# A hand-ordered head for an attention and MLP block: staged weights, stepwise transposes, sliced MLP weights

## The chip, the cores and the metric

The kernel runs on one core of a Trainium2 chip. The metric is the device time of one launch in microseconds, and smaller is better. The engines are called as the profile calls them: PE (TensorE), DVE (VectorE), ACT (ScalarE), POOL (GpSimd) and SP (SyncE, which here issues nearly all DMAs).

## The reference

```python
x = A_x                                   # 1 x 2048 x 640
xn = _layernorm(x)
return x + _A_ref(xn, A_wqkv, A_wo) + _B_ref(xn, B_w1, B_b1, B_w2, B_b2)

def _A_ref(x, wqkv, wo):                  # 32 heads of 20
    q, k, v = split(x @ wqkv)
    p = softmax(q k^T * 20 ** -0.5)
    return (p v) @ wo

def _B_ref(x, w1, b1, w2, b2):            # 640 -> 1536 -> 640
    y = _layernorm(x)
    return _gelu(y @ w1 + b1) @ w2 + b2
```

Everything is float32. An attention block and an MLP block run on the same normalized tokens, and both are added to the input.

## The kernel before, in words

The kernel has two stages. In the *head*, tokens are normalized, transposed and projected to q, k and v, and all weights are prepared. In the *attention* stage, scores, exponentials and products with v run while the MLP and the output projection are fed in between in small pieces, in an order written out by hand (`tc.manual_schedule()`).

A float32 operand is held as a pair of float16 halves, high and low, and a product is three float16 passes (`PASS`). To split a weight matrix, its squares are summed on ACT (`squares`, L94), the sum over partitions is taken by an fp32 product with a matrix of ones on PE (`mxp`, L107, in `pow2`), a power of two is made of it by six small operations on DVE, and then `split` scales (ACT, L128), casts (DVE, L129) and subtracts (DVE, L130), row by row. The matrix wqkv is loaded to one tile `wt` and split in its own place; so are w1 (`w1t`) and w2 (`w2t`) of the MLP.

The head works on four chunks `c` of 512 tokens. For each chunk there are:

- `load_x`: four tiles `xt` of 128 tokens (five buffers in all).
- `norm` (L201 to L214): statistics and scaling on DVE; the two inverse roots come from POOL (`pow`, L186) with a Newton step on DVE. A row of scales goes to `rscr`.
- `transp` (L231 to L236): 20 transposes on PE into PSUM tiles `pt`; ACT takes the high half, DVE the low half, into `xnt`, which also goes to `xscr` in DRAM for the MLP.
- `qk` (five steps `tt`, L252): 30 products into a PSUM tile `qkp`. ACT and DVE evacuate it into a buffer `qkhl` (L261, L262; two buffers), DVE squares it (`sq`, L264), and SP stores the two halves to `qkscr` (L266).
- `lengths` (L287): eight small products of `sq` for each step, from which the largest lengths of q and k are taken; `shifts` turns them into the shifts of the exponents (`brow`, `bscr`) in chunk 3.
- `vproj` (four tiles, L316): 30 products each into `vp`, evacuated into `vfull`.

`qkp`, `pt`, `vp`, and later the scores, share three PSUM buffers (tag `s`).

`residual` (L218, L219) copies x to `accscr` in DRAM and then adds b2 with an accumulating DMA issued by POOL. It stands in the text at the head of chunk 2. In the head the order of the text is no order of the engines: a planner sorts the instructions of each engine by its own estimates. So w1 is prepared in the text after chunk 1, w2 after chunk 2 (`prep`), while the planner may put their parts and the residual elsewhere.

At the end of the attention stage, `finish` of the last unit adds the two parts of its output (L639), multiplies, splits and stores them (`oscr`), with `W1` and `W2` counting the steps of the output projection (`z`, L803, evacuated at L764) that are put in between in the written order. The projection works on pieces of 256 tokens; pieces 4 to 7 need the last unit.

Of the kernel before, what the change touches and what calls it, by code (L numbers as in the profile page):

```python
# [42 lines left out]
def mha_mlp_kernel(tc, x, wqkv, wo, w1, b1, w2, b2, out):  # L43
# [4 lines left out]
    with (  # L48
# [52 lines left out]
        def pow2(acc, tag):  # L101

            lo = keep.tile([P, 1], F32, name=f"lo_{tag}")
            hi = keep.tile([P, 1], F32, name=f"hi_{tag}")
            pt = psS.tile([P, 2, 512], F32, tag="s", name="mxp")[:, 0, :]
            n = acc.shape[1]
            nc.tensor.matmul(pt[:, :n], ones, acc, start=True, stop=True)  # L107
# [11 lines left out]
        def prep(tag, ws, junk):  # L119
            pw[tag] = pow2(squares(ws, junk), tag)  # L120
            s = keep.tile([P, 1], F32, name=f"s_{tag}")
            nc.vector.tensor_scalar(s, pw[tag][1], 4096.0, None, ALU.mult)
            return s

# [8 lines left out]
        with tc.tile_pool(name="pa", bufs=2) as pa, tc.tile_pool(name="pa1", bufs=1) as pa1:  # L133
            wt = pa1.tile([P, KD, 3 * D], F32, name="wt")
            wv = wt.bitcast(F16).rearrange("p k (q s n) -> p k q s n", q=3, s=2)
# [9 lines left out]

            load_x(0)
            for q in range(2):
                for k0, k1 in ((0, 3), (3, KD)):
                    nc.sync.dma_start(wt[:, k0:k1, q * D : (q + 1) * D], wqkv_v[:, k0:k1, q * D : (q + 1) * D])
            nc.sync.dma_start(wt[:, :, 2 * D :], wqkv_v[:, :, 2 * D :])  # L150
            load_x(1)
            make_identity(nc, ident)
            nhalf = keep.tile([P, 4], F32, name="nhalf")
            half = keep.tile([H, 1], F32, name="half")
            nc.gpsimd.memset(nhalf, -0.5)
            nc.gpsimd.memset(half, 0.5)
            nc.gpsimd.memset(ones, 1.0)
# [20 lines left out]
            nc.gpsimd.memset(brow, KROW)  # L178
            nc.sync.dma_start(bscr[H : H + 1, :], brow[0:1, :])
            nc.sync.dma_start(b1t, b1.rearrange("(k p) -> p k", p=P))  # L180
            nc.sync.dma_start(w1t, w1.rearrange("(k p) n -> p k n", p=P))
            nc.sync.dma_start(w2t, w2.rearrange("(k p) n -> p k n", p=P))

            def rsqrt(dst, v, pref):
                t = pa.tile([P, 4], F32, tag=pref + "t", name=pref + "t")
                nc.gpsimd.tensor_tensor(dst, v, nhalf, ALU.pow)  # L186
# [5 lines left out]
            def norm(c):  # L192
# [11 lines left out]
                rsqrt(r, ve, "a")  # L204

                nc.vector.tensor_mul(ve, r, r)
                nc.vector.tensor_mul(ve, ve, mv[:, :, 1])
                nc.vector.tensor_scalar(ve, ve, EPS, None, ALU.add)
                nc.vector.tensor_scalar(r, r, 1024.0, None, ALU.mult)
                for j in range(4):  # L210
                    nc.vector.tensor_scalar(xt[j], xt[j], mv[:, j, 0:1], r[:, j : j + 1],
                                            ALU.subtract, ALU.mult)
                rsqrt(r2, ve, "b")
# [9 lines left out]
            def transp(c):  # L223
                xt = xts.pop(c)
                xnt = pa.tile([P, KD, 2, 512], F16, tag="xnt", name=f"xnt{c}")
                for k0 in range(0, KD, 2):
                    nk = min(2, KD - k0)
                    pt = psS.tile([P, 2, 512], F32, tag="s", name="pt")
                    for k in range(nk):
                        for j in range(4):  # L230
                            nc.tensor.transpose(pt[:, k, j * P : (j + 1) * P],  # L231
                                                xt[j][:, (k0 + k) * P : (k0 + k + 1) * P], ident)
                    ks = slice(k0, k0 + nk)
                    nc.scalar.activation(xnt[:, ks, 0, :], pt[:, :nk], AF.Copy)
                    nc.vector.tensor_sub(xnt[:, ks, 1, :], pt[:, :nk], xnt[:, ks, 0, :])
                nc.sync.dma_start(xscr[:, :, :, c * 512 : (c + 1) * 512], xnt)  # L236
                xnts[c] = xnt
# [3 lines left out]
            norms = []  # L241

            def qk(c, tt):
                xnt = xnts[c]
                ps = psS.tile([P, 2, 512], F32, tag="s", name="qkp")
                for i in range(2):
                    m = 2 * tt + i
                    q, mm = divmod(m, KD)
                    n = 0
                    for k in range(KD):  # L250
                        for a, b in PASS:
                            nc.tensor.matmul(ps[:, i, :], wv[:, k, q, a, mm * P : (mm + 1) * P],  # L252
                                             xnt[:, k, b, :], start=(n == 0), stop=(n == 3 * KD - 1))
                            n += 1
                hl = stp.tile([P, 2, 2, 512], F16, tag="ks", name="qkhl")
# [8 lines left out]
                nc.vector.tensor_mul(sq, hl[:, 0], hl[:, 0])  # L264
                for s in range(2):
                    nc.sync.dma_start(  # L266
                        qkscr[s, 2 * tt * P : (2 * tt + 2) * P, c * 512 : (c + 1) * 512]
                        .rearrange("(i p) t -> p i t", p=P), hl[:, s])

                for i in range(2):  # L270
                    q, mm = divmod(2 * tt + i, KD)
                    if mm == 0:
                        if q == 0:
                            norms.clear()
                            norms.append(psO.tile([P, 512], F32, tag="o", name="norms"))
                            norms.append(psM.tile([P, 512], F32, tag="m", name="norms"))
                    pend.append((norms[q], mm, sq, i, q, c))

            pend = []

            def lengths(last=0):
                todo = pend[: len(pend) - last]
                del pend[: len(todo)]
                for ns, mm, sq, i, q, c in todo:
                    for r in range(4):

                        nc.tensor.matmul(ns[32 * r : 32 * r + 32, :P], heads[:, mm, :],  # L287
                                         sq[:, i, r * P : (r + 1) * P], start=(mm == 0), stop=(mm == KD - 1),
                                         skip_group_check=True)
                    if mm == KD - 1:  # L290
                        nc.vector.tensor_reduce(lmx[:, q, c : c + 1], ns[:, :P], AX.X, ALU.max)
# [16 lines left out]
            def vproj(c, js):  # L308
                xnt = xnts[c]
                for j in js:  # L310
                    ps = psS.tile([P, 2, 512], F32, tag="s", name="vp")
                    for hf in range(2):
                        n = 0
                        for k in range(KD):
                            for a, b in PASS:
                                nc.tensor.matmul(ps[:, hf, :320], xnt[:, k, a, j * P : (j + 1) * P],  # L316
                                                 wv[:, k, 2, b, hf * 320 : (hf + 1) * 320],
                                                 start=(n == 0), stop=(n == 3 * KD - 1))
                                n += 1
                    kb = 4 * c + j  # L320
                    pv_ = ps[:, :, :320].rearrange("p f (h d) -> p f h d", d=DH)
                    vs = (V16 if SPLIT[kb] else V32)[:, kb].rearrange("p (f h) d -> p f h d", f=2)
                    nc.scalar.activation(vs[:, :, :, :DH], pv_, AF.Copy, scale=2.0**-14)  # L323
                    if SPLIT[kb]:
                        nc.vector.scalar_tensor_tensor(vs[:, :, :, VW : VW + DH], pv_, 2.0**-14, vs[:, :, :, :DH],
                                                       ALU.mult, ALU.subtract)

            qks = pa1.tile([P, 2], F32, name="qks")
            junk = pa1.tile([P, 3 * D], BF16, name="junk")

            def prep_qkv(q):
                c0, c1 = q * D, (q + 1) * D
                s = prep("qkv"[q], [wt[:, 0:3, c0:c1], wt[:, 3:, c0:c1]], junk)
                if q < 2:
                    nc.vector.tensor_scalar(qks[:, q : q + 1], pw["qkv"[q]][0], QKTOP, 2.0**-22, ALU.min, ALU.mult)
# [3 lines left out]
            norm(0)  # L339
            transp(0)  # L340
            prep_qkv(0)
            for c in range(4):
                if c + 2 < 4:
# [3 lines left out]
                for tt in range(3):  # L347
                    if c == 0 and tt == 2:
                        prep_qkv(1)
                        norm(1)  # L350
                    qk(c, tt)
                    lengths(2)
                if c == 0:
                    prep_qkv(2)
                if c + 1 < 4:
                    transp(c + 1)
                for tt in range(3, 5):
                    qk(c, tt)
# [633 lines left out]
```

## Time and profile before

| | us |
|---|---|
| median of 3 runs | 1438.71 (1435.95 to 1442.88) |
| profiled execution | 1444.0 |
| its span | 1442.3 |

| engine | busy us | share of the span | instructions |
|---|---|---|---|
| PE | 1348.2 | 93% | 11607 |
| DVE | 1066.4 | 74% | 1445 |
| ACT | 1122.4 | 78% | 1277 |
| POOL | 22.0 | 2% | 60 |

One execution on the chip was taken by the hardware profiler; the span goes from its first to its last instruction. In the rows that follow, a group of instructions is given as line, engine, operation, output and inputs by the kernel's names, shapes, count, busy time, mean ns of one, and the idle time of the engine just before them with what ended it. A row of a timeline begins with its start and duration. A row of a table of stretches has start and end, length, and then for each engine the busy time and the count, the granted clock of PE, the share of the DMA engines and GB/s. A row of waits says who waited for whom: total us, times, the longest. PEld is the loading of weights into PE. The digits of the page are tenths in 40 slices of the span.

### The profile page before, as it was taken

The page shows a single profiled execution, that of the slowest core. Times are in us where ns is not written, and L with a number is a line of the kernel's source. Part 1 is how long each engine was busy: PE and PEld are TensorE (multiplying, and loading weights), DVE is VectorE, ACT ScalarE, POOL GpSimd, SP SyncE. Part 2 cuts the span into 40 slices and gives each one's busy share as a digit, 9 for nine tenths or more (in the row PEclk, how much of TensorE's full clock was granted, in tenths as well). Part 3 has the DMA queues.
Part 4 walks back from the last instruction along what each step waited for, and adds up shares of the span by engine and source line. Part 5 has one row for each costly group of instructions (what it writes and reads, how often), then busy time and mean ns, then how long its engine had stood idle before and what let it go on. Part 6 is the DMA issues. An engine that isn't in the chain of part 4 may idle for free.

```text
span 1442.3 us, 28893 instructions
## 1 busy us (share of the span) xinstructions
PE 1348.2 (93%) x11607; PEld 588.6 (41%) x11607; DVE 1066.4 (74%) x1445; ACT 1122.4 (78%) x1277; POOL 22.0 (2%) x60
## 2 busy tenths in 40 slices
PE   5795599999999999999999999999999999999988
PEld 2352345534433333343343433333433433333465
DVE  6731374489977898788889778887889898788632
ACT  4731143299999989999999999899999999999600
POOL 3010000000000000000000000000000000000000
PEclk9997799999999999999999999999999999999999
DMA  9999621211111321112321113221113212242275
GB/s 356 198 238 143 114 88 37 83 52 31 54 48 49 94 82 59 32 58 55 93 75 49 47 39 107 65 79 32 58 54 102 79 56 63 74 143 65 90 205 182
DMA packets 92159, 130.90 MB, mean 91 GB/s; under 512 B 16665, under 2 KB 58329, under 8 KB 91938
## 3 DMA queue, kind: packets, MB, share of 16 engines
q1 hardware_dynamic: 89298, 122.38, 29.4%
q0 software_dynamic: 2064, 5.24, 3.3%
q8 instruction: 93, 1.52, 0.4%
q10 hardware_dynamic: 656, 1.36, 0.3%
q14 instruction: 48, 0.39, 0.1%
HBM read 86.09 MB, written 53.34 MB: 97 GB/s over the span
## 4 chain that ended last, share of the span: by engine, by line
PE 66%; DVE 14%; DMA 6%; issue 6%; ACT 4%; SPq 2%; POOL 0%; DVEq 0%; ACTq 0%; POOLq 0%
PE o L529 22%; PE s L498 14%; PE py L726 9%; PE pu L699 8%; PE qkp L252 5%; DVE low L512 5%; PE z L803 4%; PE vp L316 4%; ACT p L500 3%; DMA accscr<-in_A_x_dram 1%; DMA oa<-opart 1%; DMA oscr<-oa 1%; DVE u L654 1%; DVE u L655 1%; DVE w L658 1%
## 5 line engine op out<-in xcount | busy, mean ns | idle before, releaser
L500 ACT ACTIVATE p<-s 128x1024 f32<-128x1024 f32 x1024 | 973.6, 1042 | 51.5 <-PE s L498 45.4
L512 DVE TENSOR_TENSOR low<-p 128x1024 f16<-128x1024 f32 x512 | 608.5, 1219 | 155.8 <-ACT p L500 155.5
L529 PE MATMUL o<-p,vfull 128*32 128x512 bf16 (+1 forms) x4096 | 432.3, 493 | 0.0
L498 PE MATMUL s<-qs,ks 61*128 61x512 f16 x2048 | 317.3, 381 | 8.9 <-ACT p L500 7.4
L498 PEld LDWEIGHTS <-ks 61*128 61x128 f16 x2048 | 63.6, 94 | 296.2 <-issue 295.1
L699 PE MATMUL pu<-xm,w1t 128*128 128x256 f16 x1440 | 179.2, 273 | 4.4 <-DVE u L654 3.6
L726 PE MATMUL py<-w2t,hT 128*128 128x320 f16 x1152 | 178.6, 300 | 2.3 <-DVE xb L671 1.7
L699 PEld LDWEIGHTS <-w1t 128*128 128x128 f16 x1440 | 130.8, 98 | 71.5 <-issue 58.0
L252 PE MATMUL qkp<-xnt,wt 128*128 128x512 f16 x600 | 141.0, 393 | 7.2 <-DVE wt L129 4.6
L726 PEld LDWEIGHTS <-hT 128*128 128x128 f16 x1152 | 102.5, 98 | 90.0 <-issue 55.9
L529 PEld LDWEIGHTS <-vfull 128*32 128x32 f16 x3072 | 61.3, 95 | 145.5 <-issue 114.5
L529 PE MATMUL o<-low,vfull 128*32 128x512 f16 x1024 | 106.6, 378 | 6.2 <-DVE low L512 6.0
L261 ACT ACTIVATE qkhl<-qkp,qks 128x1024 f16<-128x1024 f32 (+1 forms) x24 | 23.2, 967 | 91.8 <-DMA qkscr<-qkhl 49.0
L252 PEld LDWEIGHTS <-wt 128*128 128x128 f16 x600 | 58.9, 101 | 83.5 <-issue 8.1
L529 PEld LDWEIGHTS o<-p,vfull 128*32 128x32 f32 x2048 | 62.5, 108 | 50.5
L803 PE MATMUL z<-w1t,ot 128*128 128x320 f16 x480 | 66.3, 299 | 3.9 <-DVE acc L764 3.3
L316 PE MATMUL vp<-wt,xnt 128*128 128x320 f16 x480 | 68.5, 306 | 0.0
L262 DVE SCALAR_TENSOR_TENSOR qkhl<-qkp,qks,qkhl 128x1024 f16<-128x1024 f32 (+1 forms) x24 | 26.4, 1101 | 46.3 <-ACT qkhl L261 46.3
L323 ACT ACTIVATE vfull<-vp 128x640 f16<-128x640 f32 (+1 forms) x16 | 11.3, 704 | 58.5 <-PE vp L316 58.5
L803 PEld LDWEIGHTS <-ot 128*128 128x128 f16 x480 | 46.5, 98 | 24.3 <-issue 4.6
L316 PEld LDWEIGHTS <-xnt 128*128 128x128 f16 x480 | 47.5, 100 | 19.9 <-issue 0.2
L764 DVE SCALAR_TENSOR_TENSOR acc<-z,sc,acc 128x320 f32<-128x320 f32 x32 | 17.4, 549 | 42.7 <-PE z L803 35.2
(161 smaller groups left out, 680.2 us busy)
## 6 DMA issues: line engine op xcount, KB each, us to landing
qkscr<-qkhl SPq DMA_DIRECT2D x40, 256.0 KB
opart<-ev SPq DMA_DIRECT2D x124, 80.0 KB
ks<-qkscr SPq DMA_DIRECT2D x120, 80.0 KB
qs<-qkscr SPq DMA_DIRECT2D x192, 40.0 KB
oa<-opart SPq DMA_DIRECT2D x32, 240.0 KB
xt<-in_A_x_dram SPq DMA_DIRECT2D x16, 320.0 KB
xscr<-xnt SPq DMA_DIRECT2D x4, 1280.0 KB
accscr<-in_B_b_dram POOLq DMA_DIRECT2D x1, 5120.0 KB, 56.7
```

The lines of the kernel that those rows point to most:

```text
L252: nc.tensor.matmul(ps[:, i, :], wv[:, k, q, a, mm * P : (mm + 1) * P], xnt[:, k, b, :], start=(n == 0), stop=(n == 3 * KD - 1))
L261: nc.scalar.activation(hl[:, 0, i0:i1], ps[:, i0:i1], AF.Copy, scale=a)
L262: nc.vector.scalar_tensor_tensor(hl[:, 1, i0:i1], ps[:, i0:i1], a, hl[:, 0, i0:i1], ALU.mult, ALU.subtract)
L316: nc.tensor.matmul(ps[:, hf, :320], xnt[:, k, a, j * P : (j + 1) * P], wv[:, k, 2, b, hf * 320 : (hf + 1) * 320], start=(n == 0), stop=(n ...
L498: nc.tensor.matmul(ps[:, a, :], ks[64 * a : 64 * a + 61, kb * P : (kb + 1) * P], qs[64 * a : 64 * a + 61, cc * 512 : (cc + 1) * 512], star ...
L500: nc.scalar.activation(pt, ps, AF.Exp, scale=QS)
L512: nc.vector.tensor_sub(low, pt, upper(pt))
L529: nc.tensor.matmul(pv.o[32 * q : 32 * q + 32, :], src[:, v0 - PAD * (1 - q % 2) :][:, :32], t, start=q not in pv.begun, stop=last, skip_gr ...
L699: nc.tensor.matmul(ps[:, i], w1v[:, k, (f + i) // 4, a, fo_ : fo_ + P], xnt[:, k, b, :], start=(n == 0), stop=(n == 3 * KD - 1))
L726: nc.tensor.matmul(ps[:, :320], hTs[mc][:, f, a, j * P : (j + 1) * P], w2v[:, f, b, hf * 320 : (hf + 1) * 320], start=(n == 0), stop=(n == ...
L764: nc.vector.scalar_tensor_tensor(acc[:, cols], ps[:, :320], fo, acc[:, cols], ALU.mult, ALU.add)
L803: nc.tensor.matmul(ps[:, :320], ot[:, k, a, j * P : (j + 1) * P], wov[:, k, b, h * 320 : (h + 1) * 320], start=(n == 0), stop=(n == 3 * KD ...
```

## The change

The head is put under `tc.manual_schedule()` too, so that each engine runs its instructions in the order of the text, and the text is rewritten:

- q, v and k of wqkv are loaded to parts of `w1t` and `w2t` (`stage`) and split from there into a tile of their own, `wv`, with two operations for a row (ACT copy with scale; DVE multiply and subtract). The loads of w2 and w1 follow on SP when the k and the v part have been split.
- `norm` is cut in three (`norm_a`, `norm_b`, `norm_c`), `transp` into steps of two blocks, with products and evacuation apart (`transp`, `transp_out`), and `qk` and `vproj` likewise (`qk_out`, `vproj_out`). The parts for the next chunk stand in the steps of this one.
- The preparation of w2 and w1 is a generator of 41 slices; one or two of them stand between the products of a step and their evacuation, from the `vproj` of chunk 0 on.
- `warm(n)` puts n fp32 products of `ones` by `ones` on PE, whose result is not used: 80 ahead of everything, 30 after the first transposes.
- In chunk 0 the squares `sq` are on ACT, later on DVE as before.
- The x tiles of chunk c + 2 are loaded, and the residual issued, after the five `qk` steps of the chunk instead of at its head.
- The sums of q and k use a PSUM tile of their own pool (`psM`) in `pow2`.
- `W2` goes from 2 to 17.

The core of the diff:

```diff
-        with tc.tile_pool(name="pa", bufs=2) as pa, tc.tile_pool(name="pa1", bufs=1) as pa1:
-            wt = pa1.tile([P, KD, 3 * D], F32, name="wt")
-            wv = wt.bitcast(F16).rearrange("p k (q s n) -> p k q s n", q=3, s=2)
+        with tc.tile_pool(name="pa", bufs=2) as pa, tc.tile_pool(name="pa1", bufs=1) as pa1, tc.manual_schedule():
+            wv = pa1.tile([P, KD, 3, 2, D], F16, name="wv")
+
+            stage = {}
+            for n, t, i in (("q", w1t, 0), ("v", w1t, 1), ("k", w2t, 0)):
+                stage[n] = (t.rearrange("p k n -> p (k n)")[:, i * KD * D : (i + 1) * KD * D]
+                            .rearrange("p (k n) -> p k n", k=KD))
...
+            def warm(n):
+
+                ps = psO.tile([P, 512], F32, tag="o", name="warm")
+                for _ in range(n):
+                    nc.tensor.matmul(ps[:, :P], ones, ones, start=True, stop=True)
...
+            def split_qkv(n):
+                q = "qkv".index(n)
                 for k in range(KD):
-                    split(pa, wt[:, k, c0:c1], wv[:, k, q, 0], wv[:, k, q, 1], s, D)
+                    nc.scalar.activation(wv[:, k, q, 0], stage[n][:, k], AF.Copy, scale=scales[n])
+                    nc.vector.scalar_tensor_tensor(wv[:, k, q, 1], stage[n][:, k], scales[n], wv[:, k, q, 0],
+                                                   ALU.mult, ALU.subtract)
...
+            def weights():
+
+                for i in range(KF // 2):
+                    if i == 0:
+                        accs["2"] = sm.tile([P, 8], F32, tag="acc2", name="acc2", bufs=1)[:, : KF // 2]
+                    nc.scalar.activation(junk[:, : 2 * D].rearrange("p (a b) -> p a b", a=2),
+                                         w2t[:, 2 * i : 2 * i + 2, :], AF.Square, accum_out=accs["2"][:, i : i + 1])
+                    yield
+                scale_of("2")
+                yield
...
+                factors()
+                yield
+                for k in range(KF):
+                    split(pa, w2t[:, k, :], w2v[:, k, 0], w2v[:, k, 1], scales["2"], D)
+                    yield
...
+            warm(80)
+            norm_a(0)
+            nc.gpsimd.memset(brow, KROW)
+            sums("q", [stage["q"][:, 0:3], stage["q"][:, 3:]])
+            norm_b(0)
+            pts = []
+            transp(0, 0, pts)
+            scale_of("q")
+            transp(0, 2, pts)
+            transp(0, 4, pts)
+            warm(30)
+            for t in pts:
+                transp_out(*t)
+            split_qkv("q")
...
             for c in range(4):
+                nxt = c + 1 if c < 3 else None
+                for tt in range(5):
+                    ps = qk(c, tt)
+                    lengths()
+
+                    if c == 0:
+                        if tt == 0:
+                            sums("k", [stage["k"][:, 0:3], stage["k"][:, 3:]])
+                            norm_c(0)
+                            norm_a(1)
+                            scale_of("k")
+                        elif tt == 1:
+                            split_qkv("k")
+                            nc.sync.dma_start(w2t, w2.rearrange("(k p) n -> p k n", p=P))
+                        elif tt == 2:
+                            sums("v", [stage["v"][:, 0:3], stage["v"][:, 3:]])
+                            norm_b(1)
+                            scale_of("v")
+                        elif tt == 3:
+                            norm_c(1)
+                            split_qkv("v")
+                            nc.sync.dma_start(w1t, w1.rearrange("(k p) n -> p k n", p=P))
+                    else:
+                        if nxt and tt < 3:
+                            (norm_a, norm_b, norm_c)[tt](nxt)
+                            some(1)
+                        else:
+                            some(2)
+                    qk_out(c, tt, ps)
+                    if nxt and tt >= 2:
+                        pts = []
+                        transp(nxt, 2 * (tt - 2), pts)
+                        transp_out(*pts[0])
                 if c + 2 < 4:
                     load_x(c + 2)
                 if c == 2:
                     residual()
-                for tt in range(3):
...
+                for j in range(4):
+                    ps = vproj(c, j)
                     lengths()
-                    shifts()
...
+                    if j == 0 and c == 3:
+                        shifts()
+                    some(2 if c < 3 else 1)
+                    vproj_out(c, j, ps)
+            some(99)
...
-            W1, W2 = 24, 2
+            W1, W2 = 24, 17
```

More of the change, by code (lines that the diff above doesn't have):

```diff
@@ L117, in mha_mlp_kernel @@
         pw = {}
[L119 to L123, printed above, removed]
         def split(pool, src, h, l, scale, n):
@@ L306, in shifts @@
                 nc.sync.dma_start(bscr[:H, :], brow)
[L308 to L326, printed above, removed]
@@ new lines, in mha_mlp_kernel, with some @@
+            slices = weights()
+            def some(n):
+                for _ in range(n):
+                    next(slices, None)
+            warm(80)
[11 more added lines that the diff above has]
+                transp_out(*t)
@@ L346, in mha_mlp_kernel @@
                     residual()
-                for tt in range(3):
[L348 to L358, printed above, removed]
-                    lengths(2)
-                if c + 2 < 4:
-                    norm(c + 2)
@@ L362, in mha_mlp_kernel @@
-                if c == 3:
-                    vproj(c, (0,))
-                    lengths()
-                    shifts()
-                    vproj(c, (1, 2, 3))
-                else:
-                    vproj(c, range(4))
-                    lengths()
-                if c == 1:
-                    s1 = prep("1", [w1t[:, k, :] for k in range(KD)], junk)
-                    for k in range(KD):
-                        for q in range(3):
-                            split(pa, w1t[:, k, q * 512 : (q + 1) * 512], w1v[:, k, q, 0], w1v[:, k, q, 1], s1, 512)
```

215 lines of the change are left out of this document (125 added, 90 removed).

## The prediction

> **What bounds the kernel now.** I read the page first: its span, its slices, and then the stretches of the head one by one.
>
> ```profile
> span 1442.3 us, 28893 instructions
> PE   5795599999999999999999999999999999999988
> DMA  9999621211111321112321113221113212242275
> ```
>
> A slice is 36 us. From the seventh on TensorE stands at 9 until the tail, so whatever this change is worth lies in the first eight slices (the head ends at 287.8) and in the last two. The profiled run took 1444.0 us, 1.7 beside the span and 5.3 above the median of 1438.7; I make the sum against 1444.0 and carry the difference over to the median.
>
> Next the busy times by stage. I cut at the first `qkp` product (22.3), at the end of each chunk's last `vp` product, and at the first and last score products of the attention.
>
> ```profile
> core 0: us, PE busy (x) PEld busy (x) DVE busy (x) ACT busy (x) POOL busy (x), PEclk, DMA share, GB/s
> 22.30:90.40 68.10, 60.12 (x326) 29.80 (x326) 49.38 (x124) 42.04 (x58) 5.08 (x4) 0.91 1.04 288
> 90.40:181.70 91.30, 58.21 (x331) 30.92 (x330) 21.43 (x44) 10.97 (x13) 4.34 (x3) 0.79 0.83 118
> 181.70:236.80 55.10, 53.23 (x333) 29.13 (x332) 30.50 (x55) 21.02 (x28) 0.00 (x0) 1.00 0.21 72
> 236.80:287.80 51.00, 51.00 (x323) 27.20 (x322) 29.35 (x56) 18.05 (x22) 0.54 (x1) 1.00 0.22 69
> 287.80:1363.00 1075.20, 1052.13 (x9765) 418.90 (x9769) 900.09 (x1080) 1021.25 (x1146) 2.04 (x3) 1.00 0.22 65
> 1363.00:1442.30 79.30, 68.47 (x515) 48.49 (x507) 23.25 (x45) 0.60 (x1) 0.00 (x0) 0.97 0.66 200
> ```
>
> The four chunks do nearly the same products, in 68.1, 91.3, 55.1 and 51.0 us. Chunk 3 has no transposes and is all TensorE; chunk 2 holds 53.2 us of TensorE work at full clock. So the head could be 3 x 53.2 + 51.0 = 210.6 us where it is 265.5. Of the 54.9 us lost, chunk 0 has 14.9, chunk 1 38.1, chunk 2 1.9. Chunk 1 is the case to explain: VectorE 21 us, ScalarE 11, but the DMA engines at 0.83. Who waits there:
>
> ```profile
> ACT qkhl L261 <- DMA qkscr<-qkhl: 44.8, 3, 20.2
> PE norms L287 <- DVE sq L264: 17.7, 1, 17.7
> PE pt L231 <- DVE xnt L235: 15.3, 1, 15.3
> ```
>
> ScalarE cannot refill a `qkhl` buffer (there are two) until its stores to `qkscr` have landed; TensorE stops behind it. What holds the stores up is the residual, which the planner had put at 74 us:
>
> ```profile
> 74.10 21.11 DMA accscr<-in_A_x_dram
> accscr<-in_B_b_dram POOLq DMA_DIRECT2D x1, 5120.0 KB, 56.7
> 98.47 4.14 SPq L266 DMA_DIRECT2D qkscr<-qkhl  x2
> 125.12 0.69 ACT L261 ACTIVATE qkhl<-qkp,qks 128x512 f16<-128x512 f32 x1 [20.21 <-DMA qkscr<-qkhl]
> q0 software_dynamic: 2064, 5.24, 82.7%
> q1 hardware_dynamic: 2460, 2.79, 16.7%
> q0 software_dynamic: 724, 1.85, 95.6%
> q1 hardware_dynamic: 500, 0.49, 11.4%
> ```
>
> The two pairs of queue rows are the DMA view of 95 to 152 us and of 104 to 120. The copy lands after 21 us, then POOL issues the accumulate (q0), and it fills the DMA engines for 56.7. A pair of stores issued at 98.5 frees its buffer at 125. Between 104 and 120 the store queue passed 500 packets, one pair (2 x 256 packets of 1 KB), while the accumulate passed 724.
>
> **The change, part by part.** (1) *The start.* PE now begins with 80 fp32 products of `ones` by `ones`, ahead of the transposes in its queue, and has 30 more between the transposes and the first `qkp`. The rows nearest to such a product:
>
> ```profile
> 12.90 4.63 PE L231 MATMUL pt<-ident,xt 128*128 128x128 f32 x20 [12.90 <-DVE xt L211]
> 13.86 3.28 PEld L231 LDWEIGHTS pt<-ident,xt 128*128 128x128 f32 x16 [0.23 <-DVE xt L211]
> 110.73 1.73 PEld L231 LDWEIGHTS pt<-ident,xt 128*128 128x128 f32 x16
> 18.20 0.38 PE L107 MATMUL mxp<-acc,ones 128*128 128x2 f32 x2 [0.67 <-DVE xnt L235]
> 22.32 16.02 PE L252 MATMUL qkp<-xnt,wt 128*128 128x512 f16 x60 [3.74 <-DVE wt L129]
> 103.92 6.65 PE L252 MATMUL qkp<-xnt,wt 128*128 128x512 f16 x30
> 128.95 9.02 PE L252 MATMUL qkp<-xnt,wt 128*128 128x512 f16 x30
> 74.01 16.47 PE L316 MATMUL vp<-wt,xnt 128*128 128x320 f16 x120
> ```
>
> One `mxp` product shows as two records, while a transpose of the same 128 columns is one. A record costs 0.108 us at full clock (1.73 / 16) and 0.205 cold (3.28 / 16), so a warm product is 0.216 or 0.41 us. The cold stretch after an idle time is worth 9.02 - 6.65 = 2.4 us, that is 4.7 us at half speed. From about 1.1 us on (`ones` is set first): 4.7 us for 11 cold products, 69 x 0.216 = 14.9, end at 20.7. The data were there at 12.9, so this is late by 8 us. Then 20 transposes (2.2) and one `mxp` (0.4), 23.3, and 30 products (6.5), 29.8. Evacuation (3 copies) and five splits fit beside these:
>
> ```profile
> L234 ACT ACTIVATE xnt<-pt 128x1024 f16<-128x1024 f32 (+1 forms) x9 | 7.9, 873 | 2.5 <-PE pt L231 2.5
> L128 ACT ACTIVATE wtmp<-w2t,s 128x640 f32<-128x640 f32 x12 | 9.6, 826 | 6.5 <-DVE w2t L130 5.4 <-DVE s L122 1.0
> L129 DVE CAST w2t<-wtmp 128x640 f16<-128x640 f32 x12 | 5.6, 486 | 0.9 <-ACT wtmp L128 0.9
> L130 DVE TENSOR_TENSOR w2t<-wtmp,w2t 128x640 f16<-128x640 f32 x12 | 9.6, 822 | 0.2
> L128 ACT ACTIVATE wtmp<-w1t,s 128x512 f32<-128x512 f32 x15 | 10.4, 717 | 7.3 <-DVE w1t L130 6.2 <-DVE s L122 1.0
> L129 DVE CAST w1t<-wtmp 128x512 f16<-128x512 f32 x15 | 6.1, 421 | 1.0 <-ACT wtmp L128 1.0
> L130 DVE TENSOR_TENSOR w1t<-wtmp,w1t 128x512 f16<-128x512 f32 x15 | 10.1, 689 | 0.3
> L94 ACT ACTIVATE junk<-w2t 128x1280 bf16<-128x1280 f32 x6 | 7.6, 1266 | 0.1
> L94 ACT ACTIVATE junk<-w1t 128x1536 bf16<-128x1536 f32 x5 | 7.4, 1478 | 0.0
> ```
>
> 3 x 0.87 + 5 x 0.83 = 6.8 us of ScalarE after the first transposes (21.6) end at 28.4, VectorE's last half 0.8 later. So `qkp` starts at about 30 instead of 22.3, but at full clock and with all of q split: the first 60 products take 13.3, not 16.0. Bounds: if a warm product were one record, the 80 would end by 13 and the start would be at about 21 (-9); cold throughout, 110 x 0.41 = 45 us, 49 (+19). The second is far off: the clock rose within 5 us in every stretch above. I take 30.
>
> (2) *Chunk 0.* A split of a q/k/v row is two operations, not three, and VectorE loses the cast (5 x 0.49 us for each matrix). The k split (5 x 0.83 on ScalarE) is queued a whole 6.65 us `qkp` step before its first use, v's two steps before, and three PSUM buffers let PE run two steps on. SP now waits for the k split with the w2 load and for the v split with the w1 load; behind each stand one pair of `qkhl` stores, which have two steps to land. Cover for all of this is the step of 6.65; without it the two splits would cost 4 us each. I leave 2.5 us for this and for scale products over the whole head.
>
> (3) *Chunks 1 and 2.* The residual is no longer in front of them: 38.1 + 1.9 us go, as does chunk 0's 14.9. The slices of MLP weights (one or two per step) stand ahead of `qkhl` on ScalarE and VectorE; chunks 2 and 3 of before hold the same splits and leave VectorE 24.6 and 21.7 us idle, so they stay hidden.
>
> (4) *The residual moves to the end of chunk 2's `qkp`.* Call T the start of chunk 3. SP issues the copy some 12 us before T (the `vp` stage, 16.5, less the last evacuations), it lands at about T + 9, and the accumulate runs to T + 65. Chunk 3's five pairs of stores fall into it, two buffers again. At 16.4 us a pair (500 packets in 16): pair 0, issued at T + 9, lands at T + 27, pair 1 at T + 43, pair 2 at T + 58; step 4 must wait for pair 2, its lengths hold PE back, and three `vp` (12.4) and a cold stretch (2.4) follow: T + 76 for 51, a stall of 25. If the queues shared evenly, 512 packets at 724 per 16 us take 11.3 us a pair: T + 63, a stall of 12. The bounds are 0 (every pair slips through) and 32 (step 4 waits for the accumulate's end: 65 + 3 + 12.4 + 2.4 - 51). I take the middle of 12 and 25, 18.5. Behind the stores SP has the stack loads, which the last three `vp` cover (12.4); behind the accumulate POOL has only the square root of the shifts, and the accumulate is issued well before that is due.
>
> The Trainium skill, "DMA: Bandwidth & Descriptors", section "Queues, rings and completion order", says that each DMA engine takes turns between the queues that have work, packet by packet. That speaks against this move, and by it the sum would use the 12 and end at 1403.6. The 724 against 500 packets agree with it only roughly.
>
> (5) *W2, 2 to 17.* At the end VectorE stands before the last unit's addition until its operands land:
>
> ```profile
> 1382.89 1.22 DVE L639 TENSOR_TENSOR oa<-oa 80x1024 f32<-80x1024 f32 x1 [6.96 <-DMA oa<-opart]
> 1384.63 8.31 PE L803 MATMUL z<-w1t,ot 128*128 128x320 f16 x60 [2.67 <-DVE acc L764]
> ```
>
> PE's 2.7 us behind it go. The store of the last unit is then late by about 3 us; piece 3 covers that (60 products of 0.137, 8.2 us), perhaps not all: -2.2, between -2.7 and +3.
>
> **Sum.** Head end: 29.8 + 210.6 + 2.5 + 18.5 = 261.4 for 287.8, -26.4. Tail -2.2. The attention between does the same work: 0. Together -28.6: 1415.4 against 1444.0, 1410.1 on the median.
>
> **Rivals.** *No second stall* (0.18): the pairs pass the accumulate, as if only the planner's order had hurt. For: between 95 and 152 q1 moved 2460 packets in all, more than q0. Against: 20 us of waiting per pair. 1410 - 18.5 = 1391.5. *Short warm-up* (0.12): one record per product, start 9 earlier, 1401. Against it is the `mxp` row. *Stores wait out the whole accumulate* (0.13): stall of 32, 1423.5. For it speak the 26 us from issue to release. *Slower: the weight slices come onto the path* (0.07). In the written order every slice stands ahead of a `qkhl`; all in a row they are 7.6 + 7.4 + 12 x 2.13 + 15 x 1.83 = 68 us, and exposed in full give 1478. It turns the sign once over 36 of the 68 show, that is if VectorE needs more than the 6.65 us of a step in most steps. Against: its idle time in chunks 2 and 3. *The order changes little* (0.05): some other transfer holds `qkhl` as now; 1438.
>
> **How the numbers follow.** Forecast 0.45, 1410. A change under 0.5% (7.2 us) cannot be told from none. Faster: 0.45 + 0.18 + 0.12 + 0.13 = 0.88; same 0.05; slower 0.07. The range takes in the four faster cases with some error of each: from 1387 (no stall, less 4.5) to 1430 (whole accumulate, plus 6.5 for chunk 0). Left out are the last two rivals, 0.12, and corners of the others.
>
> **What would show it.** Right: 60 to 80 records of `warm` before the first `pt` and the first `qkp` near 30; chunks 1 and 2 within 56 us each; `qkhl` waiting for `qkscr` in chunk 3 alone, some 20 us of PE idle there, the DMA row at 9 around it; first `s` at about 261; the 2.67 us before `z` gone. Wrong: first `qkp` before 24 (step 1), chunk 3 at 51 (step 4), PE gaps released by VectorE or ScalarE slices in chunk 1 or 2 (step 3), or a longer attention.

## The result, and the profile after

The changed kernel took 1415.4 us (median of 4 runs, 1414.5 to 1416.3) where the kernel before took 1440.6 beside it on the same chip: a ratio of 0.983, with a 95% interval of 0.980 to 0.986. The profiled execution took 1415.95 us with a span of 1414.2, against 1444.0 and 1442.3 before, so 28.1 us went in the profile and 25.2 by the medians. The forecast was 28.6.

The page of the changed kernel, with the lines that answer to those of before:

```profile
span 1414.2 us, 29326 instructions
PE   9999995899999999999999999999999999999998
DMA  7565399411112321112222113211213222241276
accscr<-in_B_b_dram POOLq DMA_DIRECT2D x1, 5120.0 KB, 54.2
```

The hole in the PE row has moved. Before, the second to fifth slices were at 7, 9, 5 and 5 ("5795599"); now only the seventh and eighth are open (5 and 8), and the DMA row has its two 9s in the sixth and seventh. The accumulate takes as long as before (54.2 us for 56.7).

The busy times by stage, cut at the first `qkp`, at the end of each chunk's last `vp`, and at the first and last products of the attention (columns as in the prediction):

```profile
core 0: us, PE busy (x) PEld busy (x) DVE busy (x) ACT busy (x) POOL busy (x), PEclk, DMA share, GB/s
0.00:30.79 30.79, 29.72 (x242) 29.71 (x243) 16.70 (x40) 12.47 (x16) 9.91 (x49) 1.00 0.77 272
30.79:83.90 53.11, 53.11 (x338) 29.50 (x336) 30.28 (x70) 35.70 (x46) 2.01 (x2) 1.00 0.65 210
83.90:137.60 53.70, 53.22 (x338) 29.45 (x337) 37.31 (x95) 24.83 (x34) 2.01 (x2) 1.00 0.55 147
137.60:190.20 52.60, 52.60 (x332) 28.87 (x330) 38.56 (x78) 20.76 (x28) 2.36 (x2) 1.00 0.49 135
190.20:260.20 70.00, 53.59 (x312) 27.85 (x309) 17.53 (x31) 10.37 (x13) 2.63 (x2) 0.90 0.82 150
260.20:1337.00 1076.80, 1052.60 (x9739) 418.53 (x9742) 896.50 (x1067) 1019.91 (x1145) 0.15 (x2) 1.00 0.22 65
1337.00:1414.20 77.20, 70.66 (x545) 49.68 (x537) 25.14 (x47) 2.04 (x3) 1.89 (x2) 0.99 0.70 211
```

Chunks 0 to 2 are now all TensorE: length and PE's busy time agree to half a microsecond, at full clock. They take 159.4 us for 214.5 before. In their place the start has grown from 22.3 to 30.8 us and chunk 3 from 51.0 to 70.0. The sum is a head of 261 us for 288. PE's timeline at the start and around the second hole:

```profile
1.07 20.82 PE L183 MATMUL warm<-ones 128*128 128x128 f32 x160 [1.07 <-POOL ones L149]
24.09 6.86 PE L183 MATMUL warm<-ones 128*128 128x128 f32 x60
30.79 6.64 PE L263 MATMUL qkp<-xnt,wv 128*128 128x512 f16 x30
231.84 0.40 PE L299 MATMUL norms<-sq,heads 128*32 128x128 bf16 x8 [8.08 <-DVE sq L284]
246.34 0.40 PE L299 MATMUL norms<-sq,heads 128*32 128x128 bf16 x8 [8.33 <-DVE sq L284]
246.67 13.57 PE L327 MATMUL vp<-wv,xnt 128*128 128x320 f16 x90
260.96 0.37 PE L581 MATMUL s<-qs,ks 61*128 61x512 f16 x1 [0.72 <-DMA qs<-bscr]
264.24 1.44 PE L581 MATMUL s<-qs,ks 61*128 61x512 f16 x5 [2.91 <-DMA ks<-bscr]
```

Behind the two waits of chunk 3 stands ACT, and behind ACT the stores. The timelines of POOL, and of ACT, in chunk 3:

```profile
199.25 2.06 POOL L231 DMA_DIRECT2D accscr<-in_B_b_dram  x1 [47.15 <-DMA accscr<-in_A_x_dram]
```

```profile
228.76 1.11 ACT L278 ACTIVATE qkhl<-qkp,qks 128x1024 f16<-128x1024 f32 x1 [16.33 <-DMA qkscr<-qkhl]
243.26 1.11 ACT L278 ACTIVATE qkhl<-qkp,qks 128x1024 f16<-128x1024 f32 x1 [13.39 <-DMA qkscr<-qkhl]
```

It is the chain of before in another place: the accumulate is issued at 199, the stores of a pair land late, `qkhl` has no free buffer, its squares `sq` come late, and PE stands at `norms`. PE had work for about half of each of ACT's waits, and stood idle for the 8 us that were left of each.

### The profile page after: what moved, and what is told of

It is laid out like the page before. It is cut to its first block, busy times and chain, and to the rows that moved or that the text cites. A ratio compares the mean times of both kernels' runs of the same rounds, so it can differ in the third digit from the quotient of the medians.

```text
span 1414.2 us, 29326 instructions
## 1 busy us (share of the span) xinstructions
PE 1365.5 (97%) x11827; PEld 613.6 (43%) x11827; DVE 1062.0 (75%) x1425; ACT 1126.1 (80%) x1282; POOL 21.0 (1%) x60
## 3 DMA queue, kind: packets, MB, share of 16 engines
q0 software_dynamic: 2064, 5.24, 2.8%
## 4 chain that ended last, share of the span: by engine, by line
PE 57%; DVE 11%; ACT 4%; DMA 3%; issue 2%; SPq 1%; DVEq 0%; ACTq 0%
PE o L612 22%; PE s L581 14%; PE py L809 9%; PE pu L782 8%; DVE low L595 5%; PE z L886 5%; ACT p L583 4%; DMA oa<-opart 1%; DMA oscr<-oa 1%; DVE u L737 1%; DVE u L738 1%; DVE w L741 1%; DVE w L742 1%; DVE hT L749 1%; ACT ev L633 1%
## 5 line engine op out<-in xcount | busy, mean ns | idle before, releaser
L263 PE MATMUL qkp<-xnt,wv 128*128 128x512 f16 x600 | 132.3, 379 | 0.0
L263 PEld LDWEIGHTS <-wv 128*128 128x128 f16 x600 | 58.2, 98 | 67.7
L327 PE MATMUL vp<-wv,xnt 128*128 128x320 f16 x480 | 69.3, 307 | 0.0
L633 ACT ACTIVATE ev<-o 128x512 f32<-128x512 f32 x64 | 39.3, 615 | 3.3 <-PE o L612 3.3
## 6 DMA issues: line engine op xcount, KB each, us to landing
accscr<-in_B_b_dram POOLq DMA_DIRECT2D x1, 5120.0 KB, 54.2
```

Of the source, the lines that this page charges most:

```text
L327: nc.tensor.matmul(ps[:, hf, :320], xnts[c][:, k, a, j * P : (j + 1) * P], wv[:, k, 2, b, hf * 320 : (hf + 1) * 320], start=(n == 0), stop ...
L633: nc.scalar.activation(evs[g, hf][:, cc], pv.o, AF.Copy)
```

## The experiments

The theory to be tested: the head is at PE's bound except for the start, which the warm products fix, and chunk 3, which waits only for the accumulating DMA. All times are medians beside runs of the kernel before on the same chip. The sets ran on four chips, on which the kernel before took 1437.3 to 1441.7, so a difference of a microsecond or two between two rows is not shown to be one.

| run | edit | us | ratio to before, 95% |
|---|---|---|---|
| e1_late | residual at the start of the attention | 1402.4 | 0.974 [0.970, 0.978] |
| e2_nob2 | no accumulating DMA (b2 left out) | 1392.6 | 0.967 [0.963, 0.972] |
| e3_before_late | kernel before, only the residual moved as in e1 | 1417.0 | 0.985 [0.980, 0.990] |
| e4_early | residual at the end of chunk 0's `qkp` | 1435.5 | 0.997 [0.995, 1.000] |
| e10_rscr | e4, one store of 4-byte pieces taken out of its way | 1424.0 | 0.989 [0.985, 0.993] |
| e5_nowarm | no warm products | 1410.8 | 0.980 [0.976, 0.983] |
| e6_shortwarm | 42 and 22 warm products | 1409.1 | 0.979 [0.975, 0.983] |
| e7_w2 | `W2` back to 2 | 1420.9 | 0.987 [0.984, 0.990] |
| e11_pool | no accumulate; POOL adds b2 in SBUF | 1401.5 | 0.973 [0.970, 0.977] |
| e12_best | e11 with 42 and 22 warm products | 1393.3 | 0.968 [0.965, 0.971] |
| e9_best | e1 with 42 and 22 warm products | 1395.6 | 0.969 [0.966, 0.972] |
| e13_pieces | e12, b2 by 16 small accumulating DMAs | 1385.3 | 0.964 [0.960, 0.968] |

**Where the second stall comes from: e1 and e2.**

```diff
 e1_late
-                if c == 2:
-                    residual()
...
                 load_chunk(0)
                 load_chunk(1)
+                residual()
 e2_nob2
-                nc.gpsimd.dma_start(accscr, b2[None, :].to_broadcast([S, D]), accum_op=ALU.add)
```

> The changed kernel with the residual (copy and accumulate) issued after the first two chunk loads of the MLP, at the start of the attention, instead of at the end of chunk 2's qkp. Theory (the accumulate's packets share the DMA engines with chunk 3's stores): chunk 3 falls from 70.0 us to 51, the first scores follow the last vp at once as they did before the change, so the 19.0 us of stall and the 3.6 us by which the attention grew both go: 1415.4 - 22.6 = 1392.8. Rival (the 54 us of accumulate cost the same wherever they lie): the stack and xm loads of the attention wait instead, and the time stays above 1405.

> The changed kernel without the accumulating DMA: b2 is left out of the sum, the copy of x stays. Theory: as with the residual in the attention, 1392.8, since the copy alone is over before chunk 3's first stores (it lands at about T + 8). If the copy, not the accumulate, holds the stores, chunk 3 stays near 70 us and the time near 1415. If this one is faster than the kernel with the late residual, the difference is what the accumulate costs in the attention.

Chunk 3 of e1 by its row of the stage table, and the longest wait of PE in e1's attention:

```profile
190.20:241.20 51.00, 51.00 (x317) 27.09 (x316) 17.76 (x32) 10.48 (x13) 0.54 (x1) 1.00 0.22 69
```

```profile
PE s L579 <- DMA ks<-bscr: 5.0, 1, 5.0
```

The first score product in PE's timeline, of e1 and of e2:

```profile
241.63 0.61 PE L579 MATMUL s<-qs,ks 61*128 61x512 f16 x4
```

```profile
240.56 0.61 PE L580 MATMUL s<-qs,ks 61*128 61x512 f16 x4
```

In both, chunk 3 takes its 51 us and the attention starts at 241, so the whole 19 us of chunk 3 belong to the residual. In e2 the copy of x is still there at the end of chunk 2's `qkp`, and the time is 1392.6 for 1392.8 expected: of the 19 us the copy costs nothing that is seen, the accumulate all. e1 came out 9.6 us above its 1392.8, short of the rival's 1405: the attention from first `s` to last `o` took 1085.0 us (241.63 to 1326.67) where e2 took 1076.8. So the accumulate costs 8 to 10 us there too. PE's wait for `ks<-bscr` is 5.0 of them; the rest was not traced to a row.

**The kernel before, with the one move: e3.**

```diff
-                if c == 2:
-                    residual()
...
                 load_chunk(1)
+                residual()
```

> The kernel before, planner and all, with only the residual moved to the start of the attention. Theory (the residual caused chunk 1's loss): the three waits of ScalarE for qkscr (44.8 us) go, chunk 1 falls from 91.3 us to about 55, and the time to 1440.6 - 36 = 1404.6, faster than the rewritten head. Rival (the planner's order is what hurts, with the residual or without): chunk 1 stays over 75 us and the gain is under 16 us.

The waits of ACT in e3's head, where before had 44.8 in three waits, and its first score product in PE's timeline:

```profile
ACT qkhl L261 <- DMA qkscr<-qkhl: 4.6, 1, 4.6
```

```profile
250.06 1.14 PE L496 MATMUL s<-qs,ks 61*128 61x512 f16 x6
```

The planner's head ends 38 us earlier, at 250 for 288. By PE's timeline chunk 1 takes 54 us for 91, while chunk 0 stays at 68: the 15 us that the changed kernel gains in chunk 0 are the rewrite's own. Of the 38 some 11 go back in the attention (1086.7 us from 250.06 to the last `o` at 1336.75, for 1076.0), so the time is 1417 and not 1405. Moving two DMAs in the old order is thus worth as much as the whole rewrite (22.4 us for 25.2, the intervals overlapping); the rewrite without that move, that is the written order with the new splits, the warm products and `W2`, is worth 14.5 us, the distance from e3 to e1, which have the residual at the same place.

**How the stores share with the accumulate: e4 and e10.**

```diff
 e4_early
-                if c == 2:
+                if c == 0:
                     residual()
 e10_rscr (on e4)
-                nc.sync.dma_start(rscr[c * 512 : (c + 1) * 512].rearrange("(j p) -> p j", p=P), r2)
+                if c == 2:
+                    held.append(r2)
+                else:
+                    store_r2(c, r2)
...
                     vproj_out(c, j, ps)
+                if c == 1:
+                    store_r2(2, held.pop())
```

> The changed kernel with the residual at the end of chunk 0's qkp instead of chunk 2's, about where the planner had put it. Theory: the same stall one or two chunks earlier. Chunk 1 grows from 53.7 us by 17 to 30, chunk 3 falls to 51, and since the attention's start is free again the total lies between 1409 and 1424. Rival (written order alone protects chunk 1): chunk 1 stays under 60 us and the time falls to about 1395.

> The kernel with the residual at the end of chunk 0's qkp, and in it one store moved: chunk 2's row of scales (rscr, 512 packets of 4 bytes, 2 KB in all) goes out after chunk 1's vp instead of in the middle of its qkp, so after the accumulate and not within it. Theory (queues take turns packet by packet, whatever a packet holds, so 512 packets of 4 bytes delay the stores behind them as much as a 512 KB pair): 1435.5 - 12 = 1423, with the long waits of chunk 1 (13.8, 3.8 and 18.0 us) shorter by about that. Rival (the share goes by bytes, or by the DMA engines' time): 2 KB do not matter, 1435 within 3 us.

ACT's and PE's waits in the head of e4, and then of e10 (where the lines are numbered 8 higher):

```profile
ACT qkhl L278 <- DMA qkscr<-qkhl: 48.4, 3, 23.8
PE norms L299 <- DVE sq L284: 35.5, 3, 18.0
```

```profile
ACT qkhl L286 <- DMA qkscr<-qkhl: 34.6, 4, 14.3
PE norms L307 <- DVE sq L292: 21.6, 3, 13.5
```

e4 came out 11.5 us above its 1409 to 1424: chunk 1 grew by 43 us (83.97 to 181.06), and not by 17 to 30. Among the pairs of stores lies the store of chunk 2's scales to `rscr`, 512 numbers written in pieces of 4 bytes. Were the engines shared by bytes, its 2 KB would be nothing beside a pair's 512 KB. Taken out of the accumulate's time it gave back 11.6 us (1435.5 to 1424.0), not much less than the 14.5 us between the landings of two pairs in the changed kernel. PE's waits fell by 13.9, nearly all of it in the last of the three. The queues of e4 from 126 to 150 us, when these small packets pass (q0 is the accumulate, q1 the stores):

```profile
q0 software_dynamic: 833, 2.13, 71.1%
q1 hardware_dynamic: 830, 0.30, 8.0%
```

The profile counts 535 packets under 512 bytes in that stretch, most of them these pieces, and still the queues pass one packet for one. With no accumulate beside it such a store is soon done: in the changed kernel 542 packets, 537 of them under 512 bytes, pass in the one microsecond from 155 to 156, behind the issue of chunk 3's row of scales at 154.6. So the turns between the two queues go by packets, whatever their size, as e10 was to show.

**The warm products: e5 and e6.**

```diff
 e5_nowarm
-            warm(80)
...
-            warm(30)
 e6_shortwarm
-            warm(80)
+            warm(42)
...
-            warm(30)
+            warm(22)
```

> The changed kernel without either warm-up (no warm products at all). Theory (80 products take 20.8 us where the tokens are normalized at 12.9, and 30 more 6.9 us): the transposes start near 12.9 at the cold rate of 0.205, the first qkp near 20 to 21 instead of 30.8, the first half of chunk 0 loses some 2.4 us to the cold clock; net 5 to 8 us faster, 1408 to 1410. Rival (the warm-up pays: cold products and splits that are not yet done cost as much as it does): 1415 within 2 us, or slower.

> The changed kernel with 42 warm products instead of 80 and 22 instead of 30. From the 20.82 us for 80 (11 cold at 0.41, then 0.235 each) 42 end at about 12.9, as the normalized tokens arrive; the first qkp comes at about 21.5 instead of 30.8 and at full clock. Theory: 1415.4 - 9 = 1406.4, and 1 to 4 us faster than without any warm-up. Rival (something else, such as the loads of k and v or the second x tiles, is then late): a gain under 5 us, with a wait of TensorE in chunk 0 that was not there.

PE's timeline of e5, and then of e6:

```profile
21.43 9.14 PE L263 MATMUL qkp<-xnt,wv 128*128 128x512 f16 x28 [0.84 <-DVE wv L361]
```

```profile
1.07 12.09 PE L183 MATMUL warm<-ones 128*128 128x128 f32 x84 [1.07 <-POOL ones L149]
21.96 6.64 PE L263 MATMUL qkp<-xnt,wv 128*128 128x512 f16 x30
224.33 0.41 PE L299 MATMUL norms<-sq,heads 128*32 128x128 bf16 x8 [9.39 <-DVE sq L284]
239.07 0.40 PE L299 MATMUL norms<-sq,heads 128*32 128x128 bf16 x8 [8.49 <-DVE sq L284]
```

With 42 products PE is through with them when the tokens are there, and `qkp` starts 8.8 us earlier at full clock. Without any, `qkp` runs cold at first (28 products in 9.14 us for 6.2, at a granted clock of 0.67 where e6's first `qkp` has 1.00). Yet e6 gained only 6.3 of its 8.8 us (1409.1, and not 1406.4): chunk 3 started 8.8 earlier and ended 5.6 earlier, its two waits longer than the changed kernel's 8.08 and 8.33. A microsecond won ahead of a stall is partly lost in it. e5, at 1410.8, came out at the edge of its 1408 to 1410. The 1.7 us between e5 and e6 lie within the spread of e5's runs (1409.0 to 1413.3), so that a short warm-up is better than none is not shown.

**The last unit: e7.**

```diff
-            W1, W2 = 24, 17
+            W1, W2 = 24, 2
```

> The changed kernel with W2 back at 2. Theory (the tail, 78.5 us before and 73.7 after from the last product of the attention, changed for this reason alone): 4 to 5 us slower, about 1420, with z waiting for acc again for 2 to 3 us and small waits for ot. Rival (the tail differs from run to run with the landing of oa): within 1.5 us of 1415.4.

The output projection in PE's timeline, of e7 and then of the changed kernel:

```profile
1363.09 8.31 PE L886 MATMUL z<-w1t,ot 128*128 128x320 f16 x60 [2.96 <-DVE acc L847]
1374.40 35.80 PE L886 MATMUL z<-w1t,ot 128*128 128x320 f16 x250 [2.22 <-DMA ot<-oscr]
```

```profile
1357.80 43.22 PE L886 MATMUL z<-w1t,ot 128*128 128x320 f16 x317
```

The changed kernel runs 317 products of `z` without a gap. `W2` is worth 5.5 us (1420.9 against 1415.4), a little more than the 4 to 5 expected: it takes away the wait behind `oa` and the one for the stored unit after it. The profiled execution of e7 is the longest of its five (1425.2), so its waits need not be the usual ones.

**A version without the accumulate: e11, e12, e9, e13.**

```diff
 e11_pool (no residual() at all)
-                    nc.sync.dma_start(xbs[0], accscr[t0 : t0 + P, :])
+                    nc.sync.dma_start(xbs[0], x2[t0 : t0 + P, :])
+                    nc.gpsimd.tensor_tensor(xbs[0], xbs[0], b2h, ALU.add)
...   (b2h is b2 as float16, loaded once before)
 e13_pieces (on e12)
-                    nc.gpsimd.tensor_tensor(xbs[0], xbs[0], b2h, ALU.add)
+                    nc.gpsimd.dma_start(xbs[0], b2[None, :].to_broadcast([P, D]), accum_op=ALU.add)
```

> The kernel after with no residual copy and no accumulating DMA: layer 2 loads its residual tile from x2 itself, and POOL adds b2 (as float16) to it in SBUF before its use. POOL has next to nothing to do in the attention and the tail. If the whole second stall is the accumulating DMA, this gives what the kernel without it gave, 1392.6 us, with b2 kept. Rival: the added step of POOL comes between the load and DVE's use of the tile and shows as waits in the last stage: above 1397.

> e11 with 42 and 22 warm products in place of 80 and 30. The shorter start was worth 8.8 us up to chunk 3, of which 3 went back in chunk 3's stall behind the accumulating DMA. Without that DMA there is no stall to give them back in: 1392.6 - 8.8 = 1383.8. Rival: the stores and the stack loads of chunk 3, or the weights, are late anyway, and 3 us or more go back: 1387 or above.

> e1 (the residual issued at the start of the attention) with 42 and 22 warm products. The stall behind the residual lies in the attention there, and its start moves with the head: 1402.4 - 8.8 = 1393.6. Rival: the residual's place in the attention gives back as much as chunk 3's stall did: 1396.6 or above.

> e12 with POOL's 16 additions in SBUF replaced by 16 accumulating DMAs of b2, each onto one residual tile of 128 x 640 in SBUF as it comes in, over the whole attention. The additions cost e11 8.9 us over the kernel without b2 (1401.5 against 1392.6), in the attention, where POOL's 1.4 us beside DVE's products of 1024 columns made those 2.2 instead of 1.2 us. With the accumulate in 16 pieces of some 3.4 us each (54 / 16), a fifth of the DMA engines in use and nobody waiting: 1393.3 - 8.9 = 1384.4. Rival: preparing the descriptors on POOL disturbs DVE as the additions did, or py's sum waits for the pieces: 1391 or above.

e11 missed by 8.9 us, on its rival's side, though not by the rival's wait. Its head ends at 240.3 as e2's does, but its attention is 8 us longer (1084.7 for 1076.8). The timelines of POOL and of DVE in e11 at one of the 16 additions:

```profile
390.35 1.40 POOL L809 TENSOR_TENSOR xb<-xb,b2h 128x640 f32<-128x640 f32 x1 [63.22 <-DMA xb<-in_A_x_dram]
```

```profile
387.18 1.22 DVE L593 TENSOR_TENSOR low<-p 128x1024 f16<-128x1024 f32 x1
390.64 2.19 DVE L593 TENSOR_TENSOR low<-p 128x1024 f16<-128x1024 f32 x1 [2.24 <-ACT p L581]
```

The DVE operation that lies beside POOL's takes 2.19 us, its neighbour 1.22; DVE's busy time over the whole kernel is 14 us more than in e2. Two of its groups of instructions between 300 and 1320 us, in e11 and then in e2, show which operations are concerned:

```profile
L736 DVE TENSOR_TENSOR u<-u,b1t 128x512 f32<-128x512 f32 x44 | 33.0, 751 | 1.5
L735 DVE TENSOR_TENSOR u<-pu,r2f 128x512 f32<-128x512 f32 x44 | 30.1, 685 | 0.7
```

```profile
L737 DVE TENSOR_TENSOR u<-u,b1t 128x512 f32<-128x512 f32 x44 | 30.5, 693 | 1.5
L736 DVE TENSOR_TENSOR u<-pu,r2f 128x512 f32<-128x512 f32 x44 | 30.2, 686 | 0.7
```

The sum of two operands in SBUF is longer in the mean (751 ns for 693), the product with `pu`, which lies in PSUM, is not (685 for 686). The Trainium skill, "SBUF — State Buffer", section "Who interferes with whom", says just this: a VectorE instruction with two SBUF inputs contends with a GpSimd instruction that reads SBUF, and one of them waits out the other. The rows above agree: POOL's addition ended at 391.75, 1.1 us after the DVE operation beside it had begun, and that one took 1.0 us longer than its neighbour. One group with a single tensor operand, the scaling to `hT`, was longer too (510 ns for 486), which that rule alone does not cover.

e12's 1383.8 was reckoned from e11's forecast and was missed with it, by 9.5 us. From e11's measured time it took 8.2 us by the shorter start (8.8 expected), where nothing stalls behind it; its rival's 1387 is passed, but because of the additions. e9 took 6.8 of its 8.8: its head ended 10.2 us earlier than e1's, and its attention was 3.4 longer, with the wait for `ks<-bscr` at 9.1 us for 5.0. Neither theory had it exactly.

e13 replaces the additions by pieces of the accumulate, one for each residual tile. Its page, the accumulating queue in the DMA view, and PE's timeline at both ends of the attention:

```profile
span 1381.6 us, 29187 instructions
DMA  8763413012123321223321123311224232342375
```

```profile
q0 software_dynamic: 2304, 5.24, 2.2%
```

```profile
231.44 0.61 PE L579 MATMUL s<-qs,ks 61*128 61x512 f16 x4
1306.53 1.03 PE L610 MATMUL o<-p,vfull 128*32 128x512 f32 x8
```

The same 5.24 MB pass the accumulating queue, no slice of the head has the DMA engines at 9, the head ends at 231.4 and the attention takes the 1076 us of before. At 1385.3 us (1384.4 expected, the rival at 1391) it beats both kernels: 52 us below the kernel before beside it, of which the changed kernel's 25 are less than half.

## Why the prediction was right, step by step

The forecast of 1410.1 for a measured 1415.4 is 5.3 us too low, of which 1.9 are the kernel before's median (1440.6 beside it, 1438.7 in the forecast) and 3.4 the drop of 25.2 for 28.6. Against the profiled execution it was 1415.4 for 1415.95, but with errors of both signs: the attention 3.6 longer than forecast, the tail 2.6 and the head 0.4 shorter.

1. *The start:* 29.8 forecast, 30.8 measured. A warm product is two records (160 for 80), so the rival of the short warm-up falls, and the 80 end at 21.9 for 20.7. The head pays for them, as e5 and e6 show.
2. *Chunk 0:* 53.2 forecast, with 2.5 more for splits and scales over the whole head; 53.1 measured, and of the 2.5 nothing is seen (chunks 0 to 2 took 159.4 for 3 x 53.2 = 159.6). The k and v splits are hidden.
3. *Chunks 1 and 2:* within 56 us forecast, 53.7 and 52.6 measured. No gap is released by a slice; the rival in which they came onto the path did not show. (By its own sum that rival would have turned the sign once 28.6 us of the slices showed; 36 is where the loss would have stood clear of the 7.2.)
4. *The second stall:* 18.5 forecast, 19.0 measured. The copy landed 9 us after chunk 3's start (199.25 against 190.2), as worked out. What came after that was not as worked out, and the size is partly luck. Pair 0 was to be caught in the accumulate and to land 27 us after the chunk's start. It slipped through: from 198 to 204 the stores' queue passed 546 packets (a pair has 512) beside 90 of the accumulate, and ACT evacuated step 2 at 210.23 without waiting for a store. Pair 1, issued at 204.5, landed 38.6 after the chunk's start, and pair 2 53.1 after it, 14.5 apart, between the even 11.3 and the 16.4 of before's trace. The queues of the changed kernel from 213 to 229:

```profile
q0 software_dynamic: 658, 1.68, 74.2%
q1 hardware_dynamic: 653, 0.63, 14.9%
```

In this stretch the share is even. This is what the Trainium skill states ("DMA: Bandwidth & Descriptors", "Queues, rings and completion order"), and e4's 833 to 830 say the same. The 724 to 500, which the prediction held against it, are a mean: in the middle of those 16 us of before, from 109 to 117, it is 325 to 303. So the rule held, but the stall of 12 that was drawn from it did not come. Two things made it longer. From 205 to 213, just after pair 1 was issued, only 81 of the stores' packets passed beside 337 of the accumulate; why they began so slowly is open. And at the pace of 653 packets in 16 us the 512 of a pair take 12.5 us, not 11.3; the 2 us from there to the 14.5 between the landings were not traced. A pair that was let through and pairs that were slower than reckoned for an even share cancelled, so that 18.5, the middle of two estimates, came out.

5. *The attention*, forecast at nothing, cost 3.6 us: 1079.6 from 260.96 to the last `o` at 1340.52, for 1076.0 before. The step that failed is "behind the stores SP has the stack loads, which the last three `vp` cover". Behind the late stores SP stood at a load of the stack until 253.07. `brow` was ready at 250.1 but was stored only at 256.07, its loads were issued at 259, and PE waited 0.72 and 2.91 us for them. Without the accumulate (e2, e13) the attention is back at 1076.
6. *The tail:* -2.2 forecast, -4.8 measured from the last `o` to the end (78.5 to 73.7); e7 has 5.5 for `W2` alone. The term was mis-sized because only the first of three gaps was counted. Before's `z` had two more behind it:

```profile
1393.57 0.45 PE L803 MATMUL z<-w1t,ot 128*128 128x320 f16 x2 [0.62 <-DVE acc L764]
1394.61 34.13 PE L803 MATMUL z<-w1t,ot 128*128 128x320 f16 x250 [0.60 <-DMA ot<-oscr]
```

All three (3.9 us) are gone, and the late store of the last unit, counted as a loss, is covered. What is left of the 4.8 and of e7's 5.5 above these 3.9 was not traced to a row.

The reason given for the gain holds, and the kernel before's loss was rightly put on the accumulate. What the prediction did not say is that most of the gain needed no rewrite: e3 has 22.4 of the 25.2 us from one move.

## What to carry to other kernels

Before an order is rewritten by hand, look for the one transfer that all waits lead to, and try it elsewhere, or in pieces, alone. The one big transfer that filled the DMA engines here had no good place among the four that were tried; cut along its consumers it stopped costing time. Time won ahead of a stall came back in full measure only where the stall was gone, so the stall goes first.

## What the runs showed of the hardware that was not expected

- A store of 512 pieces of 4 bytes beside the accumulate cost 11.6 us (e4 to e10): with a busy second queue a packet costs its turn, not its bytes (833 packets passed beside 830 in 24 us). With no accumulate beside it such a store passed in about 1 us.
- One accumulating DMA of 5.24 MB took 53 to 57 us wherever it lay and held back what was loaded or stored beside it. In the 16 pieces of e13 the same bytes cost nothing that is seen: the attention took the 1076 us of e2, which has no accumulate.
- POOL's addition in SBUF lengthened the DVE operation beside it from 1.22 to 2.19 us, and 16 such additions cost 8.9 us. With POOL's 16 DMA issues in their place (e13) the attention was as long as before.
